# Where a row of inverse roots is turned, and which engine scales two blocks of the attention

## The chip, the cores and the metric

The kernel runs on one core of a Trainium2 chip. A core has five engines that run side by side, each through its own list of instructions in order: TensorE (PE in the profile; its weight loads are PEld) multiplies matrices and writes only to PSUM, VectorE (DVE), ScalarE (ACT) and GpSimd (POOL) work on tiles, and SyncE (SP) issues the transfers from and to the chip's main memory. They wait for one another by semaphores. The metric is the device time of one execution in microseconds.

## The reference

Attention over eight batches of 576 positions with eight heads of width 64, then a gated feed-forward layer over all 4608 positions.

```python
scores = scale * np.matmul(q, k.transpose(0, 1, 3, 2))
mask_plain = (rel >= 0) & (rel < window)                                   # heads 0 to 3, window 32
mask_dil = (rel >= 0) & (rel < window * dilation) & (rel % dilation == 0)  # heads 4 to 7, dilation 4
scores = scores - np.max(scores, axis=-1, keepdims=True)
attn = np.exp(scores)
attn = attn / (np.sum(attn, axis=-1, keepdims=True) + 1e-09)
...
rms = np.sqrt(np.mean(x * x, axis=-1, keepdims=True) + 1e-06)
xn = x / rms * rms_g
g = xn @ w_gate
silu = g * (1.0 / (1.0 + np.exp(-g)))
val = xn @ w_val
return (silu * val @ w_out).astype(np.float32)
```

The attention's output, laid out as 4608 rows of 512, is x of the second part. All is float32. Two places matter here: the division of a row of exponentials by its sum, and the inverse root of the mean square by which a row of x is multiplied.

## The kernel before

**Units.** The work is cut into 16 units of 288 positions, half a batch each. While the feed-forward of unit u runs, the attention of unit u+1 is woven into it. x is held transposed, features on partitions and positions along the row, in four tiles `xraw` (c = 0 to 3) of 128 x 288.

**Three products.** From unit 1 on every feed-forward product is taken as three matmuls of a rounded high part and a low part (`three`, L725 and L728). Such parts are made by a cast on ScalarE (xhi, hhi, hi parts of q, k and v) and a subtraction on VectorE or GpSimd (xlo, hlo, low parts).

**Steps.** A unit's feed-forward has 36 steps, three for each of its 12 column blocks j: gate, val, proj. I count them from 0, and the last ones of the unit before as -1, -2 and so on. At the start of a step `flush` hands out what was put off to it by `later(steps, rank, function)`, in the order of rank; then TensorE's matmuls of the step are written. Each engine keeps the order in which the instructions are written, so rank is the order on each engine within a step. In the step behind a gate product come the tanh on ScalarE (L765, rank 0) and the silu on VectorE (L770, rank 0.6), in the step behind val the product with it on VectorE (L783, rank 0), the cast of h (L794) and its low part on GpSimd (L795, both rank 0.5). The tanh writes a tile `th` of which there is one, so it waits for the low part of the h before.

**Attention blocks.** A unit has 14 blocks (u, c, i), two heads each: three for c = 0 and 1, four for c = 2 and 3. From unit 3 on the scores of the 14 blocks stand at steps -11, -9, -7, up to 15. For a block whose scores stand at step n, VectorE takes the maximum in step n+1 (L381 and L386, rank 0.7), ScalarE the exponential with its sum in step n+2 (L401), VectorE the sum and its reciprocal in step n+4 (L410 and L411, rank -1), and right behind them GpSimd multiplies both heads' rows by the reciprocal (L417, one instruction a head). TensorE transposes the block at step n+6 (L504); ScalarE casts it out of PSUM and VectorE makes its low part (L484, L486); at step n+10 it is multiplied with v (L519). So the first block (c = 0, i = 0) is scaled in step -7, the second in -5, the third in -3. The transposed block shares the PSUM banks of gate and val, which a later gate or val must wait for.

**q and k.** Raw q and k come by transfers, are cast on ScalarE (L349, L358) and get their low parts on GpSimd (L354, L363).

**The inverse root.** For units 2 to 15 `fold(u)` in step -9 turns the tile of squared x in blocks of 32 x 32 on VectorE (L601) and sums it (L603). What remains is put off: ScalarE gathers four pieces onto 32 partitions and VectorE takes the mean (step -8), GpSimd raises it to the power -0.5 (L615, step -7, rank 0.6), ScalarE copies it out to 128 partitions (L619, step -5, rank 0.3), and VectorE turns it again into a row on every partition (L623, step -5, rank 0.62), which ScalarE copies into PSUM (L625). VectorE multiplies x by it and by the gain (L688, `normal`): c = 0 in step -5 at rank 0.75, c = 1 and 2 in step -4, c = 3 in step -3. `part(c)` casts x to its high part on ScalarE and takes the low part on VectorE (odd c) or GpSimd (even c), in steps -4 to -1 (L705, L706, rank 0.6, and 0.45 for c = 3). The exponential of a block whose scores follow a gate step stands at rank 0.42, the others at rank 2; casts of k and q stand at ranks 3 and 3.1, low parts of k at 5 and of q at 0.9.

Of the kernel before, what the change touches and what calls it, by code (L numbers as in the profile page):

```python
# [20 lines left out]
P = 128  # L21
# [41 lines left out]
def geometry(u, c):  # L63


    half = u % 2
    if c < NC // 2:
        if half:
            return [(QB * i, QB * i, 0, P) for i in range(U // QB)], QB, U + W
        return [(QB * i, max(QB * i - W, 0), 0 if i else W, P if i else QB)  # L70
                for i in range(U // QB)], QB, U
    nq = U // DIL
    keys = nq + (W if half else 0)
    return [(nq * r, keys * r, 0 if half else W, keys) for r in range(DIL)], nq, keys * DIL
# [3 lines left out]
def attn_moe(ctx: ExitStack, tc: tile.TileContext, qk_in, v_in, w_gate, w_val, w_out, rms_g, outT):  # L78
# [41 lines left out]
    def later(dt, rank, fn):  # L120
        put_off.setdefault(now[0] + dt, []).append((rank, fn))
# [274 lines left out]
    def scores_exp(u, c, i):  # L396
# [3 lines left out]
        for a in range(2):  # L400
            A.activation(out=t[:nq, a, :n], in_=t[:nq, a, :n], func=AF.Exp, scale=-1.0,  # L401
                         bias=sm[:nq, a, 0:1], accum_out=None if by_rows(u, c, i) else sm[:nq, a, 1:2])

    def scores_norm(u, c, i):
        blocks, nq, _ = geometry(u, c)
        n = blocks[i][3]
        t, sm = st[u, c, i]
        if by_rows(u, c, i):
            V.tensor_reduce(out=sm[:nq, :, 1], in_=t[:nq, :, :n], axis=mybir.AxisListType.X, op=ALU.add)
        V.tensor_reduce(out=sm[:nq, :, 3], in_=sm[:nq, :, 1:3], axis=mybir.AxisListType.X, op=ALU.add)  # L410
        V.reciprocal(out=sm[:nq, :, 3], in_=sm[:nq, :, 3])  # L411
        for a in range(2):
            if u == 1:
                later(1, -0.5, lambda a=a: A.activation(out=t[:nq, a, :n], in_=t[:nq, a, :n], func=AF.Copy,
                                                        scale=sm[:nq, a, 3:4]))
                continue
            (V if u == 0 and (c, i) > (NC - 1, 1) else G).tensor_scalar(  # L417
                out=t[:nq, a, :n], in0=t[:nq, a, :n], scalar1=sm[:nq, a, 3:4],
                scalar2=1.0, op0=ALU.mult, op1=ALU.mult)
# [71 lines left out]
    def products(q, t, o, t_ps, s_tag="s", o_tag="o", wait=0):  # L491


        if q:
            s_ps = ps.tile([P, 512], F32, tag=s_tag, name=f"s_{q[0]}_{q[1]}_{q[2]}")
        if o:
            o_ps = ps.tile([P, 512], F32, tag=o_tag, name=f"o_{o[0]}_{o[1]}_{o[2]}")
            pt = st.pop(o)
        if t:
            p, _ = st.pop(t)  # L500
        def transposed(a):
            blocks, nq, _ = geometry(*t[:2])
            n = blocks[t[2]][3]
            PE.transpose(t_ps[:n, a * QB:a * QB + nq], p[:nq, a, :n], ident[:nq, :nq])  # L504

        def output(a):
            blocks, nq, _ = geometry(*o[:2])
            n = blocks[o[2]][3]
            if o[0] < NEX:
                if o[0] == 0:  # L510
                    PE.matmul(o_ps[a * D:(a + 1) * D, :nq], vs[o][:n, a], pt[:n, 0, a, :nq], start=True, stop=True)
                    return
                if a:
                    return
                out = o_ps[:, :2 * nq].rearrange("d (a q) -> d a q", a=2)
                PE.matmul(out, vs.pop(o)[:n].rearrange("k a d -> k (a d)"), pt[:n, 0, :, :nq], start=True, stop=True)
                return
            vp = vparts[everything.index(o) % 2]
            PE.matmul(o_ps[:, 2 * a * nq:2 * (a + 1) * nq].rearrange("d (t q) -> d t q", t=2),  # L519
                      vp[:n, a].rearrange("k t d -> k (t d)"), pt[:n, :, a, :nq], start=True, stop=True)  # L520

        def scored(a):
            blocks, nq, _ = geometry(*q[:2])
            qc, kc, _, n = blocks[q[2]]
            sv = s_ps[:QB].rearrange("q (a t k) -> q a t k", a=2, t=2)
            if q[0] < NEX:
                qk = heads[q[0], 2 * q[1] + a]
                PE.matmul(sv[:nq, a, 0, :n], qk[:, qc:qc + nq], qk[:, U + kc:U + kc + n], start=True, stop=True)
                return
            qs, ks = heads[q[0], 2 * q[1] + a]  # L530
            PE.matmul(sv[:nq, a, :, :n], qs[:, qc:qc + nq], ks[:, :, kc:kc + n], start=True, stop=True)  # L531

        order = ((t, transposed), (o, output), (q, scored))
        if t and t[0] >= NEX:
            order = ((o, output), (t, transposed), (q, scored))
        parts = [(b, fn, a) for b, fn in order for a in range(2)]
        for b, fn, a in parts:
            if b:
                fn(a)
        if t:  # L540
            later(1, 0.2, lambda: untranspose(t, t_ps, wait))
        if o:
            if o[0] < NEX or wait:
                later(1, 0.41 if o[0] < NEX else 0.55, lambda: take(*o, o_ps))
            else:
                for a in range(2):
                    later(1, (0.1, 0.3)[a], lambda a=a: take(*o, o_ps, (a,)))
            if o[0] >= NEX and o[1:] == (NC - 1, len(geometry(*o[:2])[0]) - 1):
                later(1, 8, lambda: square(*o[:2]))
            if o[0] < NEX:  # L550
                later(1, 9, lambda: load_v(further(o, 3)))
            far = further(o, 2)
            if far and far[0] >= NEX:
                split_v(far, 8 if o[0] < NEX else 1)
        if q:
            later(1, 0.7, lambda: scores_max(*q, s_ps))
            behind = q == (1, 0, 2)
            later(3 if behind else 2, 0.3 if behind else 0.42 if wait == 1 else 2, lambda: scores_exp(*q))
            later(3 if q[0] < NNAT else 4, 1 if behind else -1, lambda: scores_norm(*q))
            u, c, i = q  # L560
            nxt = after(u, 2 * c, 2)
            nb = len(geometry(u, c)[0])
            if u < NEX:
                if u == NNAT - 1 and c == NC - 1 and i == nb - 1:
                    for h in range(4):
                        later(1, 9, lambda h=h: load(NNAT, h))
                if u >= NNAT and i == nb - 1 and c < NC - 1:
                    for a in range(2):
                        later(1, 9, lambda a=a: load(*after(u, 2 * c + a, 4)))
                if u == NEX - 1 and c == NC - 1 and i == nb - 1:  # L570
                    for a in range(2):
                        later(3 + a, 9, lambda a=a: split(NEX, a, (1, 2, 2, 3), G, G))
            elif nxt and i == 0:
                split(*nxt, (1, 2, 2, 3), G, G)
                split(nxt[0], nxt[1] + 1, (2, 3, 3, 4) if c < NC - 1 else (1, 2, 3, 4), G, G)
# [22 lines left out]
    def fold(u):  # L598
        nt = U // 32
        turned = sb.tile([P, U], F32, tag="tmp", name=f"sqt_{u}", bufs=2)  # L600
        V.transpose(out=turned, in_=xsq[u])  # L601
        r = sb.tile([P, 4, nt], F32, tag="rst", name=f"rst_{u}", bufs=1)
        V.tensor_reduce(out=r[:, 0], in_=turned.rearrange("p (b j) -> p b j", j=32), axis=mybir.AxisListType.X, op=ALU.add)  # L603
        g = sb.tile([P, nt], F32, tag="rroot", name=f"rroot_{u}", bufs=1)

        def gather():
            for k in range(1, 4):
                A.copy(out=r[:32, k], in_=r[32 * k:32 * (k + 1), 0])

        def mean():  # L610
            V.tensor_reduce(out=g[:32], in_=r[:32].rearrange("p k b -> p b k"), axis=mybir.AxisListType.X, op=ALU.add)
            V.tensor_scalar(out=g[:32], in0=g[:32], scalar1=1.0 / DM, scalar2=1e-6, op0=ALU.mult, op1=ALU.add)

        def root_of():
            G.tensor_tensor(out=g[:32], in0=g[:32], in1=mhalf[:32], op=ALU.pow)  # L615

        def scatter():
            for n in (32, 64):
                A.copy(out=g[n:2 * n], in_=g[:n])  # L619

        def spread():
            root = sb.tile([P, U], F32, tag="tmp", name=f"root_{u}", bufs=2)
            V.transpose(out=root.rearrange("p (b j) -> p b j", j=32), in_=g[:, :, None].to_broadcast([P, nt, 32]))  # L623
            rst[u] = ps.tile([P, U], F32, tag="o", name=f"bps_{u}")
            A.copy(out=rst[u], in_=root)  # L625

        later(1, 0.65, gather)
        later(1, 0.9, mean)
        later(2, 0.6, root_of)
        later(4, 0.3, scatter)  # L630
        later(4, 0.62, spread)

# [367 lines left out]
```

## Time and profile before

| | us |
|---|---|
| median of 3 runs | 1109.67 (1109.3 to 1109.92) |
| the profiled execution's own time | 1111.93 |
| span of its instructions | 1110.1 |
| granted TensorE clock, mean | 0.998 |

The profile is of one execution. A row of a timeline reads: start and duration in us, engine, line of the kernel, operation, the tile written and the tiles read, partitions x elements, the count of instructions merged into the row, and in brackets how long the engine had been idle and what ended that. A row of grouped instructions reads: line, engine, operation, tiles and shapes, count, busy us and mean ns of one, then the idle time before them. Busy times of engines other than the one that sets the end cost nothing by themselves. The end of a matmul is modelled (0.30 us of duration, though one follows the other every 0.13 us), so TensorE's noted idle time is shorter than the time it lost.

### The profile page before, as it was taken

How to read it: one execution, taken by the hardware profiler on the slowest of the kernel's cores; microseconds unless marked ns; L12 is line 12 of the kernel's file. 1: busy time of each engine (PE TensorE's matmuls, PEld its weight loads, DVE VectorE, ACT ScalarE, POOL GpSimd, SP SyncE). 2: the span in 40 equal slices, each digit the busy share in tenths (PEclk: the TensorE clock that was granted, in tenths of full speed). 3: DMA queues.
4: the chain of work that ended last, by engine and by line, in shares of the span. 5: the costliest groups of instructions: out<-in, count | busy, mean ns of one | idle time of the engine just before them, and what ended most of it. 6: DMA issues, size and time to landing. Idle time of an engine off the chain costs nothing.

```text
span 1110.1 us, 25458 instructions
## 1 busy us (share of the span) xinstructions
PE 1096.9 (99%) x8304; PEld 1067.3 (96%) x8304; DVE 805.0 (73%) x3135; ACT 619.7 (56%) x2244; POOL 673.1 (61%) x1124
## 2 busy tenths in 40 slices
PE   8999999999999999999999999999999999999998
PEld 7787999999999999999999999999999999999998
DVE  6889667868687786877768687786868768687411
ACT  6794676546465564646556464564647556464311
POOL 6333588657586675757657585675757657584311
PEclk9999999999999999999999999999999999999999
DMA  9664212212121121311212121131212212120000
GB/s 258 192 249 181 74 51 80 84 35 81 42 92 50 43 86 40 94 40 55 83 39 84 41 84 54 48 94 29 89 43 77 68 32 80 49 79 14 15 8 22
DMA packets 61542, 82.16 MB, mean 74 GB/s; under 512 B 7298, under 2 KB 41090, under 8 KB 61410
## 3 DMA queue, kind: packets, MB, share of 16 engines
q1 hardware_dynamic: 61410, 80.54, 24.0%
q8 instruction: 66, 1.08, 0.4%
q14 instruction: 66, 0.54, 0.2%
HBM read 71.08 MB, written 9.44 MB: 73 GB/s over the span
## 4 chain that ended last, share of the span: by engine, by line
PE 77%; DVE 10%; ACT 5%; POOL 4%; issue 4%; DMA 0%; DVEq 0%; POOLq 0%; ACTq 0%; SPq 0%
PE acc L728 14%; PE g L728 14%; PE v L728 13%; PE acc L725 7%; PE g L725 7%; PE v L725 7%; PE o L519 3%; PE s L531 2%; ACT t L401 2%; PE t L504 2%; DVE t L386 2%; PE acc L722 1%; DVE t L381 1%; DVE th L770 1%; PE g L722 1%
## 5 line engine op out<-in xcount | busy, mean ns | idle before, releaser
L795 POOL TENSOR_TENSOR hlo<-th,hhi 128x288 fp32r<-128x288 f32 x179 | 144.9, 810 | 172.7 <-ACT hhi L794 155.3
L401 ACT ACTIVATE t<-t,sum 96x128 f32<-96x128 f32 (+3 forms) x448 | 166.1, 374 | 101.5 <-DVE sum L386 96.7
L728 PE MATMUL acc<-hhi,lo 128*128 128x288 f32 x720 | 212.5, 295 | 0.0
L417 POOL TENSOR_SCALAR t<-t,sum 96x128 f32<-96x128 f32 (+3 forms) x416 | 150.4, 374 | 98.2 <-DVE sum L411 84.0
L765 ACT ACTIVATE th<-g 128x288 f32<-128x288 f32 x180 | 73.9, 410 | 210.2 <-PE g L728 121.4
L728 PE MATMUL v<-xhi,lo 128*128 128x288 f32 x612 | 181.0, 296 | 0.0
L728 PE MATMUL g<-xhi,lo 128*128 128x288 f32 x612 | 181.0, 296 | 0.0
L439 DVE TENSOR_REDUCE xraw<-o 64x72 f32<-64x144 f32 (+1 forms) x364 | 116.9, 321 | 84.0 <-PE o L519 80.6
L770 DVE SCALAR_TENSOR_TENSOR th<-th,g 128x288 f32<-128x288 f32 x180 | 80.8, 449 | 94.0 <-ACT th L765 75.0
L728 PEld LDWEIGHTS acc<-hhi,lo 128*128 128x128 f32 x720 | 135.3, 188 | 0.0
L324 POOL TENSOR_TENSOR vhl<-vt,vhl 128x128 fp32r<-128x128 f32 x182 | 84.3, 463 | 72.8 <-ACT vhl L320 69.6
L794 ACT CAST hhi<-th 128x288 fp32r<-128x288 f32 x180 | 77.6, 431 | 77.0 <-DVE th L783 76.9
L728 PEld LDWEIGHTS v<-xhi,lo 128*128 128x128 f32 x612 | 115.2, 188 | 0.0
L728 PEld LDWEIGHTS g<-xhi,lo 128*128 128x128 f32 x612 | 115.1, 188 | 0.0
L441 DVE TENSOR_TENSOR xraw<-o,xraw 64x72 f32<-64x72 f32 (+1 forms) x364 | 101.1, 278 | 12.5
L725 PE MATMUL acc<-hhi,hi_o 128*128 128x288 f32 x360 | 108.2, 300 | 0.0
L725 PE MATMUL g<-xhi,hi_g 128*128 128x288 f32 x357 | 107.5, 301 | 0.0
L783 DVE TENSOR_TENSOR th<-th,v 128x288 f32<-128x288 f32 x180 | 79.7, 443 | 37.4 <-PE v L728 35.5
L728 PE MATMUL acc<-hlo,hi_o 128*128 128x288 f32 x360 | 106.5, 296 | 0.0
L363 POOL TENSOR_TENSOR qs<-qk,qs 64x288 fp32r<-64x288 f32 x104 | 84.0, 807 | 19.6 <-ACT qs L358 12.3
L728 PE MATMUL g<-xlo,hi_g 128*128 128x288 f32 x322 | 95.4, 296 | 0.0
L354 POOL TENSOR_TENSOR ks<-qk,ks 128x288 fp32r<-128x288 f32 (+2 forms) x104 | 93.3, 902 | 3.1
(200 smaller groups left out, 3476.5 us busy)
## 6 DMA issues: line engine op xcount, KB each, us to landing
qk<-in_qk_dram SPq DMA_DIRECT2D x60, 288.0 KB, 2.8
vt<-in_v_dram SPq DMA_DIRECT2D x196, 64.0 KB, 1.9
qk<-in_qk_dram SPq DMA_DIRECT2D x30, 352.0 KB, 2.9
out_dram<-ot SPq DMA_DIRECT2D x64, 144.0 KB, 1.9
qk<-in_qk_dram SPq DMA_DIRECT2D x30, 304.0 KB, 2.8
raw<-in_w_gate_dram SPq DMA_DIRECT2D x12, 512.0 KB, 4.2
raw<-in_w_val_dram SPq DMA_DIRECT2D x12, 512.0 KB, 3.3
raw<-in_w_out_dram SPq DMA_DIRECT2D x12, 512.0 KB, 4.2
```

Of the source, the lines that this page charges most:

```text
L324: G.tensor_tensor(out=vp[:, :, 1], in0=vs.pop(b), in1=vp[:, :, 0], op=ALU.subtract)
L354: ek.tensor_tensor(out=ks[:, 1, :nkt], in0=kr, in1=ks[:, 0, :nkt], op=ALU.subtract)
L363: eq.tensor_tensor(out=qs[D:], in0=qr[D:], in1=qs[D:], op=ALU.subtract)
L401: A.activation(out=t[:nq, a, :n], in_=t[:nq, a, :n], func=AF.Exp, scale=-1.0, bias=sm[:nq, a, 0:1], accum_out=None if by_rows(u, c, i) els ...
L417: (V if u == 0 and (c, i) > (NC - 1, 1) else G).tensor_scalar(out=t[:nq, a, :n], in0=t[:nq, a, :n], scalar1=sm[:nq, a, 3:4], scalar2=1.0, ...
L439: V.tensor_reduce(out=ours, in_=o[:D, cols:cols + 2 * nq].rearrange("d (t q) -> d q t", t=2), axis=mybir.AxisListType.X, op=ALU.add)
L441: V.tensor_tensor(out=ours, in0=o[D:, cols:cols + nq], in1=ours, op=ALU.add)
L725: PE.matmul(out, wh[:, cc, :], xh, start=start, stop=False)
L728: PE.matmul(out, w[:, cc, :], v, start=False, stop=stop and k == 1)
L770: V.scalar_tensor_tensor(out=t, in0=t, scalar=1.0, in1=g, op0=ALU.add, op1=ALU.mult)
L783: V.tensor_tensor(out=t, in0=t, in1=v_ps[:, :U], op=ALU.mult)
L795: (V if (u, j) == (NU - 1, NJ - 1) else G).tensor_tensor(out=lo, in0=t, in1=hi, op=ALU.subtract)
```

## The change

Three edits. The second turn writes its tile in PSUM itself, and the tile in SBUF and ScalarE's copy go. The power moves from rank 0.6 to 0.45 of its step, ahead of the low part of h (0.5). From unit 3 on the first and the third block of c = 0 are multiplied by their reciprocals on ScalarE, at rank 0.55 of the step in which GpSimd did it; the sum and the reciprocal stay on VectorE at rank -1.

```diff
+    def by_scalar(u, c, i):
+        return u >= NEX and c == 0 and i != 1
+
+    def scores_scaled(u, c, i):
+        _, nq, _ = geometry(u, c)
+        n = geometry(u, c)[0][i][3]
+        t, sm = st[u, c, i]
+        for a in range(2):
+            A.activation(out=t[:nq, a, :n], in_=t[:nq, a, :n], func=AF.Copy, scale=sm[:nq, a, 3:4])
+
     def scores_norm(u, c, i):
...
         V.reciprocal(out=sm[:nq, :, 3], in_=sm[:nq, :, 3])
+        if by_scalar(u, c, i):
+            return
         for a in range(2):
...
             later(3 if q[0] < NNAT else 4, 1 if behind else -1, lambda: scores_norm(*q))
+            if by_scalar(*q):
+                later(4, 0.55, lambda: scores_scaled(*q))
...
         def spread():
-            root = sb.tile([P, U], F32, tag="tmp", name=f"root_{u}", bufs=2)
-            V.transpose(out=root.rearrange("p (b j) -> p b j", j=32), in_=g[:, :, None].to_broadcast([P, nt, 32]))
             rst[u] = ps.tile([P, U], F32, tag="o", name=f"bps_{u}")
-            A.copy(out=rst[u], in_=root)
+            V.transpose(out=rst[u].rearrange("p (b j) -> p b j", j=32), in_=g[:, :, None].to_broadcast([P, nt, 32]))
...
-        later(2, 0.6, root_of)
+        later(2, 0.45, root_of)
```

## The prediction

> **What bounds the kernel now.** The page comes first: its busy shares and its chain of waits.
>
> ```profile
> PE 1096.9 (99%) x8304; PEld 1067.3 (96%) x8304; DVE 805.0 (73%) x3135; ACT 619.7 (56%) x2244; POOL 673.1 (61%) x1124
> PE 77%; DVE 10%; ACT 5%; POOL 4%; issue 4%; DMA 0%; DVEq 0%; POOLq 0%; ACTq 0%; SPq 0%
> ```
>
> TensorE is busy 99% of the span. A unit's work on VectorE, ScalarE and GpSimd can only matter where TensorE stands for it, so the second view is the waits of TensorE (us in total, times, longest; PEld is its weight load).
>
> ```profile
> PEld t L504 <- DVE th L770: 5.3, 13, 0.4
> PEld v L725 <- DVE pt L486: 4.7, 8, 0.6
> ```
>
> About 10 us in all: 8 waits of the first val group of a unit for the low part of a transposed block, 13 waits of a transpose for a silu. That is the most that work around the root can give. Third, the timeline of one engine at a time around a unit's start. In the unit with the big waits (I call these units heavy; they alternate with light ones) TensorE begins val at 454.58, when L486 has ended (454.17 + 0.36 = 454.53). In a light unit the val begins at 388.08, L486 ends at 387.67 + 0.36 = 388.03, and no idle time is noted: no loss, but no slack either.
>
> ```profile
> 454.58 0.40 PE L725 MATMUL v<-xhi,hi_g 128*128 128x288 f32 x1 [0.40 <-DVE pt L486]
> 454.17 0.36 DVE L486 TENSOR_TENSOR pt<-t,pt 128x192 fp32r<-128x192 f32 x1
> ...
> 388.08 0.40 PE L725 MATMUL v<-xhi,hi_g 128*128 128x288 f32 x1
> 387.67 0.36 DVE L486 TENSOR_TENSOR pt<-t,pt 128x192 fp32r<-128x192 f32 x1
> ```
>
> So whatever moves that L486 later, moves TensorE later by the same, in both kinds. The 10 us of the two waits are the ceiling of a gain; a loss has none.
>
> **What leads to that L486 in a heavy unit**, engine by engine, ahead of it in time:
>
> ```profile
> 443.05 0.41 ACT L765 ACTIVATE th<-g 128x288 f32<-128x288 f32 x1 [1.88 <-PE g L728]
> 443.86 0.43 ACT L619 COPY rroot<-rroot 32x9 f32<-32x9 f32 x2 [0.39 <-POOL rroot L615]
> 444.88 0.40 ACT L625 COPY bps<-root 128x288 f32<-128x288 f32 x1 [0.60 <-DVE root L623]
> 447.41 0.43 ACT L705 CAST xhi<-xraw 128x288 fp32r<-128x288 f32 x1
> 449.60 0.30 ACT L484 CAST pt<-g 128x192 fp32r<-128x192 f32 x1
> 449.80 0.44 ACT L705 CAST xhi<-xraw 128x288 fp32r<-128x288 f32 x1
> 451.14 0.40 ACT L401 ACTIVATE t<-t,sum 96x128 f32<-96x128 f32 x1 [0.58 <-DVE sum L386]
> 451.93 0.41 ACT L705 CAST xhi<-xraw 128x288 fp32r<-128x288 f32 x1
> ...
> 443.50 0.45 DVE L770 SCALAR_TENSOR_TENSOR th<-th,g 128x288 f32<-128x288 f32 x1 [0.86 <-ACT th L765]
> 444.37 0.48 DVE L623 STREAM_TRANSPOSE root<-rroot 128x288 f32<-128x288 f32 x1 [0.42 <-ACT rroot L619]
> 445.32 0.52 DVE L688 SCALAR_TENSOR_TENSOR xraw<-xraw,gs,bps 128x288 f32<-128x288 f32 x1 [0.47 <-ACT bps L625]
> 448.03 0.17 DVE L411 RECIPROCAL sum<-sum 96x2 f32<-96x2 f32 x1
> 450.00 0.45 DVE L770 SCALAR_TENSOR_TENSOR th<-th,g 128x288 f32<-128x288 f32 x1 [0.76 <-POOL t L417]
> 452.38 1.20 DVE L706 TENSOR_TENSOR xlo<-xraw,xhi 128x288 fp32r<-128x288 f32 x1 [0.18 <-ACT xhi L705]
> ...
> 440.46 0.72 POOL L417 TENSOR_SCALAR t<-t,sum 96x128 f32<-96x128 f32 x2 [0.44 <-DVE sum L411]
> 441.26 0.80 POOL L795 TENSOR_TENSOR hlo<-th,hhi 128x288 fp32r<-128x288 f32 x1
> 442.02 1.80 POOL L615 TENSOR_TENSOR rroot<-rroot,mhalf 32x9 f32<-32x9 f32 x1
> 448.37 1.03 POOL L417 TENSOR_SCALAR t<-t,sum 96x128 f32<-96x128 f32 x2
> 449.37 1.08 POOL L354 TENSOR_TENSOR ks<-qk,ks 128x416 fp32r<-128x416 f32 x1
> 450.41 0.80 POOL L706 TENSOR_TENSOR xlo<-xraw,xhi 128x288 fp32r<-128x288 f32 x1
> 452.17 1.09 POOL L354 TENSOR_TENSOR ks<-qk,ks 128x416 fp32r<-128x416 f32 x1
> ```
>
> Read it as one chain. The power (442.02) ends at 443.82, ScalarE spreads it (443.86), VectorE turns it (444.37), ScalarE copies it (444.88), VectorE normalises x (445.32). From there VectorE runs without a break to the third block's reciprocal, which ends at 448.20. ScalarE runs without a break from 444.88 to 450.57, with the casts of x (447.41, 449.80) and the tanh and the low part's source (449.60) one behind the other. The silu of 450.00 starts 0.10 us after that cast ends (449.90), whatever the note says: the note names POOL's L417, which was over at 449.40. Behind the silu come the next block's scores, its exp at 451.14 (ScalarE idle for 0.58 until then), the last cast of x (451.93), its low part (452.38), and then the output halves and L486. So the end of this chain is set by how late ScalarE is at 447.41 to 449.90.
>
> **The change, part by part.**
>
> *Turn into PSUM.* It removes 14 turns into SBUF and 14 copies:
>
> ```profile
> L623 DVE STREAM_TRANSPOSE root<-rroot 128x288 f32<-128x288 f32 x14 | 6.7, 478 | 5.0 <-ACT rroot L619 5.0
> L625 ACT COPY bps<-root 128x288 f32<-128x288 f32 x14 | 5.7, 404 | 8.4 <-DVE root L623 8.4
> ```
>
> and adds 14 turns into PSUM. No VectorE write of PSUM stands in the trace. Its bounds are ScalarE's copy of this shape into PSUM, 0.40 us, and the slowest undisturbed VectorE row of the shape, 0.52 (L688); I take 0.48, the turn as it is, since it differs only in where it writes. Normalising then starts 0.03 us behind the turn rather than 0.47 behind it: 0.43 earlier. ScalarE loses 0.40 of work and a stand of 0.60. The Trainium skill ("ScalarE: Activation LUTs", Step-by-step: what each stage is for) says that ScalarE lies closer to PSUM and VectorE closer to SBUF, which speaks against the new place; it prices no VectorE write, and by it the sum would go to the upper end, about 0.5 us in all. No run here shows it yet.
>
> *Power ahead of h's low part, first block's scaling off GpSimd.* Ahead of the power stand the two scalings of the first block (440.46, 0.72) and the low part (441.26, 0.80); both go, so it starts some 1.5 us or more earlier and ends about 442.0 or 442.3. The low part of h is then done about 442.8 to 443.1; the tanh that overwrites its source starts at 443.05, so at worst it slips by 0.1, which I cost at nothing. The spread now waits for nothing but its place behind the tanh: 443.48 rather than 443.86, and VectorE's turn comes right behind its silu, 443.50 + 0.45 + 0.03 = 443.98 rather than 444.37: 0.39 earlier. The first block's two scalings on ScalarE stand where it is idle (the 1.88 us before 443.05): nothing. With the turn's 0.43 the VectorE chain is 0.82 us earlier: normalising at 444.50, third reciprocal ending at 448.20 - 0.82 = 447.38.
>
> *Third block on ScalarE.* Its two scalings leave GpSimd (448.37, 1.03) and go onto ScalarE in the same step, rank 0.55, that is **ahead of the second cast of x** (rank 0.6, now at 447.41), of the next exp, of two casts of k and q, and of the tanh. In order, ScalarE meets them when it is through with the casts that follow VectorE's earlier chain, 447.41 - 0.82 = 446.59, and must stand until the reciprocal at 447.38. Today ScalarE passes this place before the reciprocal (447.41 against 448.20), since it has no business with it. The price of a pair is in unit 1's rows:
>
> ```profile
> 42.16 0.69 ACT L414 ACTIVATE t<-t,sum 96x128 f32<-96x128 f32 x2 [1.09 <-DVE sum L411]
> 42.76 0.39 ACT L765 ACTIVATE h<-g 128x288 f32<-128x288 f32 x1
> ```
>
> 0.69 us for two, the next instruction 0.60 after the first. So the cast of x comes at 447.38 + 0.04 + 0.60 = 448.02, **0.61 us later** than now, in spite of the earlier root. Nothing between it and the silu of 450.00 waits for anything else, so the silu, the scores, the exp and the last cast come 0.6 later too. The low part of 452.38 takes 1.20 us rather than 0.44, and ends 0.32 after GpSimd's L354 (453.26); I read it as waiting for that one. L354 hangs on the L706 of 450.41, which began 0.17 after its own cast ended (449.80 + 0.44): some of that is slack, and I take half of it off. So L486 and val come **0.52 us later** in a heavy unit. The Trainium skill ("SBUF — State Buffer", Who interferes with whom) has the rule: a VectorE instruction with two SBUF inputs and a GpSimd one that reads SBUF lock each other out; the row agrees. Without it the sum would take 0.61.
>
> A light unit, by the same steps:
>
> ```profile
> 377.99 0.43 ACT L619 COPY rroot<-rroot 32x9 f32<-32x9 f32 x2 [0.24 <-POOL rroot L615]
> 382.02 0.16 DVE L411 RECIPROCAL sum<-sum 96x2 f32<-96x2 f32 x1
> 381.44 0.43 ACT L705 CAST xhi<-xraw 128x288 fp32r<-128x288 f32 x1
> ```
>
> The spread gains 0.22, the turn 0.43; the reciprocal ends at 382.18 - 0.65 = 381.53, the cast comes at 381.53 + 0.64 = 382.17 rather than 381.44: **0.72 later**, with no slack. Two units differ:
>
> ```profile
> 177.65 0.45 DVE L770 SCALAR_TENSOR_TENSOR th<-th,g 128x288 f32<-128x288 f32 x1 [1.29 <-ACT th L765]
> 182.31 0.43 ACT L705 CAST xhi<-xraw 128x288 fp32r<-128x288 f32 x1
> 515.52 0.43 ACT L349 CAST ks<-qk 128x288 fp32r<-128x288 f32 x1 [0.41 <-DMA qk<-in_qk_dram]
> ```
>
> In the first heavy one the power is later, so more is gained: silu at 177.65, normalising 1.00 behind it, reciprocal 2.71 + 0.17 behind that, cast 0.64 later at 182.17, 0.14 earlier than now. In one light unit ScalarE stands 0.41 for a DMA, which takes up that much: 0.3. The last root (the fourteenth) has no next unit's blocks beside it: 0.
>
> **Sum**: 6 heavy x 0.52 + 5 light x 0.72 + 0.3 - 0.14 = 6.9 us. The profiled execution takes 1111.93 us (span 1110.1), so 1118.8 in its own time; the median of the runs is 2.3 lower, 1109.67, and I put the same difference on it: **1116.6 us**. The bounds: turn 0.40 to 0.52 (-1.0 to +0.5 over 12 such units), scaling pair 0.50 to 0.70 in ScalarE's queue (-1.2 to +1.2), slack in heavy units (-0.5 to +0.5): the forecast's own range is 1114 to 1119.
>
> **Rivals.**
>
> *Faster: the root's 0.82 us comes through.* If ScalarE doesn't stand at the third block's scaling, or what it delays isn't what L486 waits for, the earlier root shortens the heavy units' wait of 0.56 (the notes' longest 0.6), and part of the 0.4 behind it: some 0.6 to 0.8 x 7 = 4 to 6 us, 1104 to 1106. Light units have no wait to lose. For it: GpSimd is freed of 1.03 us just ahead of L354, and runs without a break from 449.37 to 453.26. Against it: L706 of 450.41 needs ScalarE's cast of 449.80, which comes later. It decides at the reciprocal: it must end 0.7 us sooner than I make it. Chance 0.17.
>
> *No difference.* The stand is there but short (the reciprocal at 446.8), or the root's gain and the pair's cost cancel as in the first heavy unit: within 2 us of 1109.67. Chance 0.18. That GpSimd's relief is hidden anyway is part of it.
>
> *Dearer still.* The write to PSUM costs more than any row of the shape, or semaphores tie the scaling to the casts behind it: 0.3 us more in 13 units, 1120 to 1122. Chance 0.05.
>
> *Forecast*: ScalarE stands at the third block's scaling, and what is queued behind it reaches TensorE, 1114 to 1119: 0.60.
>
> A measurement of this kernel tells about 0.2%, 2.2 us, from no change. Faster 0.17, same 0.18, slower 0.65. The range leaves out the faster rival and the far end: 1107.5 to 1121; the likeliest case's own range is 1114 to 1119.
>
> **What would show it.** Right: the third block's scaling on ScalarE preceded by an idle time that VectorE's L411 ends, some 0.5 to 0.8 us, once a unit; the second cast of x 0.6 us later against the tanh at the unit's step; TensorE's wait for L486 thirteen times rather than eight, 1.0 us in heavy units, 0.7 in light ones. The turn itself about 0.48, normalising right behind it. Wrong: no idle time before the scaling, or the silu no later; then the waits for L486 shrink and the first rival holds.

## The result and the profile after

| | before | after |
|---|---|---|
| median of the runs, us | 1109.51 (1109.3 to 1109.92) | 1117.38 (1116.03 to 1118.35) |
| ratio to before | | 1.0070, 95% interval 1.0052 to 1.0087 |
| own time of the profiled execution | 1111.93 | 1116.75 |
| span of its instructions | 1110.1 | 1115.0 |

The changed kernel is slower by 0.7%. First the page, its busy shares and its chain of waits:

```profile
PE 1097.7 (98%) x8304; PEld 1065.3 (96%) x8304; DVE 805.4 (72%) x3135; ACT 631.6 (57%) x2282; POOL 650.4 (58%) x1072
PE 78%; DVE 11%; ACT 5%; issue 3%; POOL 1%; DMA 1%; SPq 0%; ACTq 0%; POOLq 0%; DVEq 0%
```

GpSimd has 22.7 us less to do, ScalarE 11.9 more, TensorE the same. No engine's sum tells why the time grew. The view of the waits does (us in total, times, longest):

```profile
ACT t L413 <- DVE sum L422: 10.6, 13, 0.8
...
PEld v L738 <- DVE pt L499: 5.9, 13, 0.6
PEld t L517 <- DVE th L783: 5.2, 13, 0.4
PEld t L517 <- ACT t L401: 5.0, 12, 0.6
```

The first row is new: 13 times, once a unit, ScalarE stands 0.8 us for VectorE's sums, ahead of a scaling (L413 is the line of `scores_scaled`, L422 the reciprocal). The second was 4.7 us in 8 waits and is 5.9 in 13. The last is new too: 12 times TensorE now stands at a transpose ahead of the unit's first val. (Lines have moved: L499 is the low part that was L486, L783 the silu, L718 and L719 the cast and the low part of x.)

The heavy unit that the prediction went through, ScalarE's timeline around the new wait, GpSimd's behind it and VectorE's:

```profile
443.23 0.41 ACT L778 ACTIVATE th<-g 128x288 f32<-128x288 f32 x1 [1.28 <-PE g L741]
...
447.62 0.70 ACT L413 ACTIVATE t<-t,sum 96x128 f32<-96x128 f32 x2 [0.84 <-DVE sum L422]
448.23 0.42 ACT L718 CAST xhi<-xraw 128x288 fp32r<-128x288 f32 x1
...
450.39 0.30 ACT L497 CAST pt<-g 128x192 fp32r<-128x192 f32 x1
```
```profile
451.11 0.81 POOL L719 TENSOR_TENSOR xlo<-xraw,xhi 128x288 fp32r<-128x288 f32 x1 [2.40 <-ACT xhi L718]
...
452.86 1.08 POOL L354 TENSOR_TENSOR ks<-qk,ks 128x416 fp32r<-128x416 f32 x1
```
```profile
444.13 0.49 DVE L638 STREAM_TRANSPOSE bps<-rroot 128x288 f32<-128x288 f32 x1
444.66 0.51 DVE L701 SCALAR_TENSOR_TENSOR xraw<-xraw,gs,bps 128x288 f32<-128x288 f32 x1
...
447.36 0.16 DVE L422 RECIPROCAL sum<-sum 96x2 f32<-96x2 f32 x1
...
450.79 0.46 DVE L783 SCALAR_TENSOR_TENSOR th<-th,g 128x288 f32<-128x288 f32 x1 [1.23 <-issue]
...
453.17 1.08 DVE L719 TENSOR_TENSOR xlo<-xraw,xhi 128x288 fp32r<-128x288 f32 x1 [0.17 <-ACT xhi L718]
```

Measured from the tanh that TensorE releases (443.05 before, 443.23 after), the reciprocal ends 4.29 us behind it, 5.15 before: the earlier root brings 0.86. The second cast of x starts 5.00 behind it, 4.36 before: 0.64 late. The silu stands at 7.56, 6.95 before: 0.61 late. So the gain arrives at VectorE and is lost on ScalarE. GpSimd, freed of the scaling, stands 2.40 us for ScalarE's cast.

What TensorE loses is read from the same matmul in consecutive units, the first of val, before and after:

```profile
322.12 0.40 PE L725 MATMUL v<-xhi,hi_g 128*128 128x288 f32 x1 [0.38 <-DVE pt L486]
```
```profile
321.57 0.41 PE L738 MATMUL v<-xhi,hi_g 128*128 128x288 f32 x1 [0.35 <-DVE pt L499]
...
388.25 0.40 PE L738 MATMUL v<-xhi,hi_g 128*128 128x288 f32 x1
...
452.53 0.36 PE L517 MATMUL t<-ident,t 96*128 96x96 f32 x2 [0.42 <-DVE sum L421]
...
455.26 0.40 PE L738 MATMUL v<-xhi,hi_g 128*128 128x288 f32 x1 [0.34 <-DVE pt L499]
```

With the rows of before at 388.08 and 454.58: the step into the light unit took 65.96 us and takes 66.68, 0.72 more; into the heavy one 66.50 and takes 67.01, 0.51 more. The row of 388.25 notes no idle time though it is late: the modelled end of the matmul ahead covers up to 0.16 us, and the rest of the delay stands a step earlier, at a transpose. In the heavy unit too the added idle time is at that transpose (452.53, 0.42; none before), while the wait at val is no longer than it was (0.34 against 0.40). What the transpose waits for is not settled: the note names VectorE's sum, the waits view ScalarE's exp, and VectorE's low part of the block ahead ended at about the same time.

Both kernels write the same 8304 matmuls in the same order, so their starts can be compared one by one. The executions also differ in the first 170 us, which the change doesn't touch: by -2.4 to +0.3 us between the profile of before and the others of this study. Two rows that are the same matmul, before and after, show it:

```profile
175.26 0.40 PE L725 MATMUL g<-xhi,hi_o 128*128 128x288 f32 x1 [0.17 <-DVE th L783]
```
```profile
173.74 0.40 PE L738 MATMUL g<-xhi,hi_o 128*128 128x288 f32 x1 [0.17 <-DVE th L796]
```

From there to the end of the span it is 934.8 us before and 941.3 after: **the change costs 6.4 us**, and this execution had started 1.5 us better. Some 1.4 of these 1.5 us arise between 30 and 40 us, and go with the granted clock: from 20 to 60 us it was 0.96 in the profile of before and 1.00 in that of after. The profiles of e4, e5, e7, e8 and e10 have the 0.96 as well and lack the 1.4 us; all others have them. In the experiments "from 170 us" is this comparison, the difference of matched matmuls at the end less that at 170 us. It doesn't carry the start's scatter.

### The profile page after: what moved, and what is told of

It reads as the page before. It is cut to its first block, busy times and chain, and to the rows that moved or that the text cites. A ratio compares the mean times of both kernels' runs of the same rounds, so it can differ in the third digit from the quotient of the medians.

```text
span 1115.0 us, 25390 instructions
## 1 busy us (share of the span) xinstructions
PE 1097.7 (98%) x8304; PEld 1065.3 (96%) x8304; DVE 805.4 (72%) x3135; ACT 631.6 (57%) x2282; POOL 650.4 (58%) x1072
## 3 DMA queue, kind: packets, MB, share of 16 engines
q8 instruction: 66, 1.08, 0.4%
## 4 chain that ended last, share of the span: by engine, by line
PE 78%; DVE 11%; ACT 5%; issue 3%; POOL 1%; DMA 1%; SPq 0%; ACTq 0%; POOLq 0%; DVEq 0%
PE acc L741 14%; PE g L741 14%; PE v L741 13%; PE acc L738 7%; PE g L738 7%; PE v L738 7%; PE o L532 3%; PE s L544 2%; ACT t L401 2%; PE acc L735 2%; PE v L735 2%; PE g L735 2%; DVE th L783 2%; DVE t L386 2%; DVE xraw L701 2%
## 5 line engine op out<-in xcount | busy, mean ns | idle before, releaser
L430 POOL TENSOR_SCALAR t<-t,sum 72x72 f32<-72x72 f32 (+3 forms) x364 | 128.4, 364 | 93.2 <-DVE sum L422 78.5
L783 DVE SCALAR_TENSOR_TENSOR th<-th,g 128x288 f32<-128x288 f32 x180 | 80.8, 449 | 99.5 <-ACT th L778 75.5
L354 POOL TENSOR_TENSOR ks<-qk,ks 128x288 fp32r<-128x288 f32 (+2 forms) x104 | 93.2, 902 | 3.1
```

The costliest lines, as they stand in the source:

```text
L354: ek.tensor_tensor(out=ks[:, 1, :nkt], in0=kr, in1=ks[:, 0, :nkt], op=ALU.subtract)
L783: V.scalar_tensor_tensor(out=t, in0=t, scalar=1.0, in1=g, op0=ALU.add, op1=ALU.mult)
```

## The experiments

The theory: ScalarE's stand at the third block's reciprocal, and the 0.60 us of scaling behind it, delay all that is queued there; the other edits gain. The rivals are named in each expectation. The diffs are against the changed kernel.

| kernel | median, us | ratio, 95% interval | from 170 us | a heavy unit | a light unit |
|---|---|---|---|---|---|
| the change | 1117.38 | 1.0052 to 1.0087 | +6.4 | +0.5 | +0.7 |
| e1 turn, power | 1108.28 | 0.9972 to 0.9992 | -2.6 | -0.2 | -0.0 |
| e2 turn, power, first block | 1098.61 | 0.9881 to 0.9911 | -11.7 | -0.65 or -1.36 | -0.6 |
| e3 third block alone | 1126.65 | 1.014 to 1.0174 | +16.7 | +1.3 | +1.4 |
| e4 third block behind all | 1105.42 | 0.9948 to 0.9974 | -4.6 | -0.3 | -0.1 |
| e5 turn alone | 1106.12 | 0.9909 to 0.997 | -4.6 | -0.5 | -0.2 |
| e6 power, first block | 1105.19 | 0.9927 to 0.9974 | -4.9 | -0.4 | -0.2 |
| e7 third block a step later | 1100.91 | 0.9879 to 0.9939 | -9.0 | -0.65 | -0.6 |
| e8 third block behind the cast | 1112.28 | 0.9994 to 1.0038 | +2.2 | +0.2 | +0.4 |
| e9 e2, last cast ahead | 1096.37 | 0.9855 to 0.9886 | -14.2 | -1.36 | -0.6 |
| e10 e7, last cast ahead | 1097.15 | 0.9855 to 0.9891 | -14.1 | -1.36 | -0.6 |

The medians of before beside them were 1110.0 (e1 to e4), 1109.81 (e5 to e8) and 1111.03 us (e9, e10). The last two columns are the typical unit; the first heavy unit and one light one, where a transfer of q and k is late, differ.

**e1: no scaling on ScalarE.**

```diff
-        return u >= NEX and c == 0 and i != 1
+        return False
```

> Turn into PSUM and power ahead, all three blocks of c = 0 scaled by GpSimd again. Theory (ScalarE's stand at the third block is the whole loss): no loss. But GpSimd now has the first block's scaling, the power (1.80) and the low part of h (0.80) in a row, so the low part ends 0.75 us later than before, the tanh that overwrites its source comes about 0.8 us later, and the earlier root is spent on that: about the kernel before, 1108 to 1111 us. Rival (VectorE's write to PSUM or the power's new place is the cost): most of the 6 to 8 us remains, 1115 or more.

Measured 1108.28 us, the loss gone. The two other edits don't carry it. Nor do they gain much, for the reason expected: GpSimd's timeline in e1's heavy unit, and ScalarE's.

```profile
437.64 0.72 POOL L430 TENSOR_SCALAR t<-t,sum 96x128 f32<-96x128 f32 x2 [0.44 <-DVE sum L422]
438.32 1.80 POOL L630 TENSOR_TENSOR rroot<-rroot,mhalf 32x9 f32<-32x9 f32 x1
440.09 0.80 POOL L808 TENSOR_TENSOR hlo<-th,hhi 128x288 fp32r<-128x288 f32 x1
```
```profile
440.92 0.41 ACT L778 ACTIVATE th<-g 128x288 f32<-128x288 f32 x1 [2.57 <-POOL hlo L808]
441.36 0.43 ACT L634 COPY rroot<-rroot 32x9 f32<-32x9 f32 x2
```

Scaling, power and low part in a row end at 440.89, and the tanh, which overwrites the low part's source, waits for that and not for TensorE.

**e2: the first block alone on ScalarE.**

```diff
-        return u >= NEX and c == 0 and i != 1
+        return u >= NEX and c == 0 and i == 0
```

> Turn into PSUM, power ahead, first block on ScalarE, third block on GpSimd. Theory: nothing stands on ScalarE, the root is 0.82 us earlier in heavy units, their wait for L486 (0.56) goes and part of the 0.39 behind it: about 1 us in each of 7 heavy units, 1101 to 1106 us; light units the same as before. Rival (the loss lies in the turn or in the first block): 1112 or more.

Measured 1098.61 us, better than expected. The first block's scaling costs ScalarE nothing that reaches TensorE, and with it off GpSimd the kernel is 9.1 us better than e1. What its new place would bring without the earlier power was not run. Two things were not expected: the light units gain 0.6 too, and the heavy ones gain 0.65 or 1.36, in no order that the schedule has. A likely cause of the latter stands in e2's own rows, VectorE and GpSimd in a unit of the one kind (446.75) and of the other (577.33):

```profile
446.75 0.46 DVE L719 TENSOR_TENSOR xlo<-xraw,xhi 128x288 fp32r<-128x288 f32 x1 [0.17 <-ACT xhi L718]
...
577.33 1.38 DVE L719 TENSOR_TENSOR xlo<-xraw,spare 128x288 fp32r<-128x288 f32 x1 [0.18 <-ACT spare L718]
```
```profile
446.75 1.41 POOL L354 TENSOR_TENSOR ks<-qk,ks 128x416 fp32r<-128x416 f32 x1
...
577.32 1.08 POOL L354 TENSOR_TENSOR ks<-qk,ks 128x416 fp32r<-128x416 f32 x1
```

They start within 0.01 us of each other. In the first unit GpSimd takes 1.41 instead of 1.08 and VectorE its plain 0.46; in the second VectorE takes 1.38, the other's 1.08 and some more. e9 tests this. In the light units VectorE has become the undisturbed one; the first row is of before, the second of e2:

```profile
386.25 0.83 DVE L706 TENSOR_TENSOR xlo<-xraw,spare 128x288 fp32r<-128x288 f32 x1 [0.17 <-ACT spare L705]
```
```profile
381.56 0.46 DVE L719 TENSOR_TENSOR xlo<-xraw,spare 128x288 fp32r<-128x288 f32 x1 [0.18 <-ACT spare L718]
```

**e3: the third block alone, all else as before.**

```diff
-        return u >= NEX and c == 0 and i != 1
+        return u >= NEX and c == 0 and i == 2
...
+            root = sb.tile([P, U], F32, tag="tmp", name=f"root_{u}", bufs=2)
+            V.transpose(out=root.rearrange("p (b j) -> p b j", j=32), in_=g[:, :, None].to_broadcast([P, nt, 32]))
             rst[u] = ps.tile([P, U], F32, tag="o", name=f"bps_{u}")
-            V.transpose(out=rst[u].rearrange("p (b j) -> p b j", j=32), in_=g[:, :, None].to_broadcast([P, nt, 32]))
+            A.copy(out=rst[u], in_=root)
...
-        later(2, 0.45, root_of)
+        later(2, 0.6, root_of)
```

> The kernel before with the third block's scaling alone on ScalarE, at rank 0.55. Theory: the root is as late as before, so ScalarE stands until the reciprocal ends at 448.20 instead of 447.38 and the second cast of x comes 448.84 instead of 447.41: 1.4 us later in each of 13 units, 17 us, 1124 to 1129 us; twice the loss of the whole change. Rival (the loss is ScalarE's added work of 0.6 us, wherever it stands): 13 x 0.6, 1115 to 1119 us.

Measured 1126.65 us; 16.7 us from 170 us on, 1.3 to 1.4 in a typical unit. The rival that the work on ScalarE costs as such (8 us) falls. e3's ScalarE:

```profile
450.87 0.70 ACT L413 ACTIVATE t<-t,sum 96x128 f32<-96x128 f32 x2 [0.78 <-DVE sum L422]
451.47 0.42 ACT L720 CAST xhi<-xraw 128x288 fp32r<-128x288 f32 x1
```

The stand is no longer than in the changed kernel, 0.78 against 0.84; the difference is that there the 0.8 us of the earlier root paid for it.

**e4, e7, e8: the same scaling at other places of ScalarE's order.** All do the same work on all engines; only the third block's place differs.

```diff
-                later(4, 0.55, lambda: scores_scaled(*q))
+                later(4, 3.5 if q[2] == 2 else 0.55, lambda: scores_scaled(*q))                # e4
+                later(*((5, 3.5) if q[2] == 2 else (4, 0.55)), lambda: scores_scaled(*q))      # e7
+                later(4, 0.65 if q[2] == 2 else 0.55, lambda: scores_scaled(*q))               # e8
```

> The changed kernel with the third block's scaling at rank 3.5 of the same step, behind the casts of x, k and q and the exp. Same work on ScalarE, but the reciprocal is long there. Theory: no stand; the casts of x come 0.8 us earlier than before the change, the tanh and what follows 0.0 to 0.2 us earlier: 1105 to 1110 us. Rival (ScalarE's added work as such): 1114 or more.

> The changed kernel with the third block's scaling one step later, rank 3.5: behind the tanh, the low part's source and the casts, where ScalarE was idle for 0.58 us before the next exp. GpSimd stays free of it. Theory: no stand, the added 0.6 us falls into idle time, and GpSimd is 1 us freer ahead of the low parts of k and x: as fast as e2 or faster, 1095 to 1100 us. Rival (third block on ScalarE costs its 0.6 us wherever it is): 1104 or more.

> The changed kernel with the third block's scaling at rank 0.65: just behind the second cast of x instead of ahead of it, still ahead of the exp and the tanh. Theory: ScalarE does the cast (0.34) and then stands for what is left, 0.4 to 0.5 us, so the tanh comes 0.3 to 0.4 us later than in the kernel before instead of 0.6 to 0.7: 1111 to 1114 us, half of the loss. Rival (what costs is the cast of x being late, not the queue behind it): 1106 or less.

Measured 1105.42, 1100.91 and 1112.28 us. In the changed kernel the scaling stands ahead of the cast (+6.4 us from 170 us), in e8 one instruction later (+2.2), in e4 behind the exp and the casts and ahead of the tanh (-4.6), in e7 behind the tanh too (-9.0). The price is that of the place. In e8 the wait is there, shorter; in e4 it is gone, and its row shows the scaling in ScalarE's unbroken run:

```profile
ACT t L413 <- DVE sum L422: 6.3, 13, 0.5
```
```profile
446.04 0.69 ACT L413 ACTIVATE t<-t,sum 96x128 f32<-96x128 f32 x2
446.63 0.39 ACT L778 ACTIVATE th<-g 128x288 f32<-128x288 f32 x1
```

The first is the waits view of e8, the second the timeline of e4. What e4 still loses against e7 I read as the 0.6 us by which the tanh stands behind the scaling: behind the same matmul it starts at 2.93 us in e4 and at 2.33 in e7. e7's median was a little above its expectation (1095 to 1100): GpSimd was first in every typical heavy unit there. e8's rival (the late cast is all that costs) falls: the cast is early in e8, 0.75 us ahead of its place before the change, and the kernel still loses 2.2 us from 170 us on, about a third of the whole loss.

**e5 and e6: the gain, split.** e5 is the changed kernel with no scaling on ScalarE and the power at rank 0.6 again; e6 is e2 with the turn into SBUF and ScalarE's copy.

```diff
-        return u >= NEX and c == 0 and i != 1
+        return False                                     # e5
+        return u >= NEX and c == 0 and i == 0            # e6
...
-        later(2, 0.45, root_of)
+        later(2, 0.6, root_of)                           # e5
...
-            V.transpose(out=rst[u].rearrange("p (b j) -> p b j", j=32), in_=g[:, :, None].to_broadcast([P, nt, 32]))
+            root = sb.tile([P, U], F32, tag="tmp", name=f"root_{u}", bufs=2)                                           # e6
+            V.transpose(out=root.rearrange("p (b j) -> p b j", j=32), in_=g[:, :, None].to_broadcast([P, nt, 32]))    # e6
+            A.copy(out=rst[u], in_=root)                                                                              # e6
```

> The kernel before with the turn into PSUM alone. Theory (the turn itself costs nothing and takes 0.43 us out of the chain from the power to the normalised x): the wait for L486 of 0.56 shrinks to 0.1 in each of 7 heavy units and the 0.39 behind it stays, 3 to 4 us less, 1105.5 to 1107.5. Rival (VectorE pays for PSUM, or loses elsewhere): 1110 or more. And the row of the turn: 0.48 by the theory, over 0.55 by the rival.

> Power ahead and first block on ScalarE, the turn into SBUF with ScalarE's copy as before, third block on GpSimd: the fast kernel e2 without its turn. Theory: 0.39 us of the 0.82 remain in heavy units, 0.22 of 0.65 in light ones, so 3 to 6 of e2's 11 us: 1104 to 1107 us. Rival (the power and the first block give all of it): 1100 or less.

Measured 1106.12 and 1105.19 us, both as expected: 4.6 and 4.9 us from 170 us on. Their sum is 9.5; together, in e2, they bring 11.7. There VectorE's low part is undisturbed (0.46 us) in the light units, 0.6 us each where e5 and e6 together bring 0.4, and in three of the six typical heavy units. The turn into PSUM, the row of e5:

```profile
L638 DVE STREAM_TRANSPOSE bps<-rroot 128x288 f32<-128x288 f32 x14 | 6.9, 494 | 5.1 <-ACT rroot L634 5.0
```

494 ns, against 478 into SBUF: 0.2 us over all 14.

**e9 and e10: the race, and the best kernel.** e9 is e2, e10 is e7, both with the last cast of x ahead of the exp, where ScalarE was idle:

```diff
-                later((2, 3, 4, 5)[c], 0.45 if c == NC - 1 and u > 1 else 0.6, lambda c=c: part(c))
+                later((2, 3, 4, 5)[c], 0.41 if c == NC - 1 and u > 1 else 0.6, lambda c=c: part(c))
```

> The fast kernel e2 (first block on ScalarE, third on GpSimd) with the last cast of x at rank 0.41 instead of 0.45, so that it stands ahead of the exp, where ScalarE was idle for 0.55 us. In e2 the low part of c = 3 on VectorE and a low part of k on GpSimd start within 0.03 us of each other: where VectorE is first it takes 0.46 us, where GpSimd is first 1.38, and the unit gains 1.36 or 0.65 us. Theory (who starts first holds the other off for a whole instruction): VectorE's now starts 0.17 us earlier, always first, 0.46 in all 13 units, and the four heavy units with 0.65 gain 0.7 more: 1094 to 1097 us. Rival (the alternation has another cause): as e2, 1097 to 1100 us, with 1.38 in every other heavy unit.

> The same edit on e7 (third block on ScalarE one step later). There GpSimd was first by 0.04 us in every heavy unit, 1.35 us. Theory: VectorE's low part now starts earlier, but the scaling already fills ScalarE's idle time, so the exp comes up to 0.3 us later; VectorE first, 0.46 us, heavy units gain up to 0.7 more than the 0.65 of e7: 1095 to 1099 us. Rival: no change against e7, 1100 to 1102 us.

Measured 1096.37 and 1097.15 us. In e9 the low part on VectorE is ahead of GpSimd's in all 13 units and takes 0.45 to 0.52 us:

```profile
575.53 0.48 DVE L719 TENSOR_TENSOR xlo<-xraw,spare 128x288 fp32r<-128x288 f32 x1
```
```profile
575.77 1.18 POOL L354 TENSOR_TENSOR ks<-qk,ks 128x416 fp32r<-128x416 f32 x1
```

Every typical heavy unit now gains 1.3 to 1.4 us. The waits of TensorE's matmuls by e9's trace are those of the start alone; the low part and the silu are gone from them, and from those of its weight loads:

```profile
PE busy L858 <- ACT ones L95: 2.4, 1, 2.4
PE t_first L517 <- POOL t L430: 0.7, 1, 0.7
PE s L541 <- DVE sum L386: 0.2, 1, 0.2
PE o L529 <- ACT xraw L448: 0.2, 1, 0.2
PE g L738 <- DVE th L796: 0.2, 1, 0.2
```

e9 beats both kernels, by 1.3% against before. It takes the turn, the power and the first block of this change and leaves the third block where it was. e10 ties with it: with the place right and the last cast ahead, the third block on ScalarE neither helps nor hurts.

## Why the prediction was right

- **The stand on ScalarE** was the step that decided, and it is there, 13 times, 0.84 us in the heavy unit where the prediction had 0.79 (446.59 to 447.38). The second cast of x came 0.64 late against 0.61 forecast, the silu 0.61 against 0.6.
- **The prices by unit**: 0.51 measured against 0.52 in a heavy unit, 0.72 against 0.72 in a light one, 0.2 against 0.3 in the one with the late transfer, -0.3 against -0.14 in the first. The sum was 6.9 and came to 6.4 in matched matmuls.
- **Where TensorE stands** was foreseen in part. It waits for the low part of the transposed block thirteen times, as forecast, but 0.6 us in a heavy unit and 0.3 in a light one instead of 1.0 and 0.7. The rest of the delay is met at the transpose a step earlier, which the prediction did not name.
- **The lock between the low part of x and L354**: in the changed kernel L719 takes 1.08 in the heavy unit (453.17 to 454.25), and the loss there is 0.51, not 0.61. It ends 0.31 behind L354 (453.94), as it ended 0.32 behind before, and L354 itself starts 0.51 later against the tanh (9.63, 9.12 before). So the reading that it waits for GpSimd's instruction holds; e2 and e9 show it from both sides. The rule of the Trainium skill ("SBUF — State Buffer", section Who interferes with whom) agrees with these rows. That half of GpSimd's slack of 0.17 would be used up was a guess without a row, and a lucky one: 0.09 is left (451.11 against 450.59 + 0.43).
- **The turn in PSUM**: 0.49 against 0.48, inside its bounds. The remark of the Trainium skill ("ScalarE: Activation LUTs", section Step-by-step: what each stage is for) that VectorE lies closer to SBUF agrees with the 16 ns that the turn takes more, which are too few to matter.
- **The power ahead** cost nothing, as long as the first block's scaling was off GpSimd: in the changed kernel the tanh still waits for TensorE (443.23). e1 shows what it costs without that cover.
- **Median**: 1116.6 forecast, 1117.38 measured. The 0.8 us are less than the runs of the changed kernel lie apart (1116.03 to 1118.35).

Wrong was one statement that carried no term of the sum: that the two noted waits, about 10 us, are the ceiling of a gain. e2 gains 11.7 us from 170 us on, e9 14.2. Noted idle time leaves out what a matmul's modelled end covers, up to 0.16 us a delay, and the matmul behind a late one is late as well. TensorE's timeline of before shows the second:

```profile
454.81 0.29 PE L728 MATMUL v<-spare,hi_g 128*128 128x288 f32 x1
454.95 0.29 PE L728 MATMUL v<-xhi,lo 128*128 128x288 f32 x1
455.07 0.29 PE L725 MATMUL v<-xhi,hi_g 128*128 128x288 f32 x1
```

The late matmul started at 454.58, so the next came 0.23 us behind it, and those after that 0.12 to 0.14 apart. And light units were misread as having no wait to lose: the 13 waits of a transpose for the silu are one a unit, light ones too. The row of before, in the light unit of 388.08:

```profile
390.37 0.37 PE L504 MATMUL t<-ident,t 96*96 96x96 f32 x2 [0.25 <-DVE th L770]
```

They gained 0.6 in e2, where VectorE's low part is also 0.37 us shorter. The one light unit of e7 in which it is not (1.07 us) gained 0.2. The rival on the faster side rested on the same bound and was sized too small; its mechanism is what e2 shows once the third block is left alone. The chance of 0.18 for no difference rested on a short stand, or on gain and cost cancelling; the stand was not short, and the two cancel in the first heavy unit alone.

## What to carry to other kernels

Work handed to an engine with time to spare is priced by its place in that engine's order: at the place chosen here it waited for a result that the engine had so far run ahead of, and 0.6 us of work cost up to 1.4 us a unit; behind the casts it cost 0.3 to 0.5 more than behind the tanh, and behind the tanh, with the last cast of x moved too, nothing (e10 against e9). Before such a move, compare when the engine passes the place with when the input is there. And where a cast can stand ahead of a wait rather than behind it, the idle time of that wait can take it, as in e9.

## What the runs showed that was not expected

- The low part of x on VectorE and that of k on GpSimd, which each read two tiles of SBUF, hold each other off, and a hundredth of a microsecond decides: 446.75 against 446.75, VectorE undisturbed at 0.46; 577.33 against 577.32, VectorE at 1.38. In e2 three of the six typical heavy units went one way and three the other, worth 0.7 us each time, in no regular turn (e9's expectation had four of one kind, alternating).
- A silu started 0.10 us behind a cast whose result it doesn't use, the one queued right behind its tanh, in the kernel before (450.00, cast ended 449.90). The changed kernel has the same (450.79 against 450.39 + 0.30), and so has every one of the 13 units. Where this cast doesn't follow the tanh, the silu starts right behind the tanh itself (443.50 against 443.05 + 0.41). Both the cast and the silu read a PSUM tile of the name `g` (the rows leave the tiles' numbers out). Whether it is that tile, or a signal that a later instruction gives for both, was not tried.
